# One kernel, two orders: the steps of a gated linear attention and its expert layer put in another sequence

## The chip, the cores and the metric

One core of one Trainium2 chip runs the whole program in one launch. The time is the device time of the program in microseconds (us), the median of several runs. The engines are PE (TensorE, matrix products; its weight loads are listed as PEld), DVE (VectorE), ACT (ScalarE), POOL (GpSimd) and SP (SyncE, which here issues DMA transfers).

## What is computed

For 4 sequences of 768 tokens and 8 heads of width 48, a state of 48 by 48 per head is decayed by a gate and updated by each token; the output of the heads is the input of a layer with 2048 hidden units and the activation h cos(h).

```python
f = 1.0 / (1.0 + np.exp(-f_logit))
for t in range(S):                                   # S = 768
    state = f[:, :, t, :, None] * state + np.einsum('bhd,bhe->bhde', k[:, :, t], v[:, :, t])
    y[:, :, t] = np.einsum('bhd,bhde->bhe', q[:, :, t], state)
x = y.transpose(0, 2, 1, 3).reshape(B * S, H * D)    # 3072 x 384
h = x @ w_in                                         # 3072 x 2048
out = (h * np.cos(h)) @ w_out                        # 3072 x 384
```

## The kernel before

**Pairs.** The tokens are cut into 12 pairs (0 to 11) of 256 tokens, three pairs for each of the 4 sequences; two chunks of 128 rows are worked on together, and each partition holds two tokens. Heads are handled in two halves of four (the `.0` and `.1` of a step's name; for pairs 0 and 1 the loads and gates are also cut into these halves, 192 KB each instead of 384 KB).

**Units.** The expert layer works on 13 units of tokens, the first two of 128 (both from pair 0), then eleven of 256 (unit m from 2 on uses pair m - 1). For a unit of 128 tokens one step of the first product covers 512 hidden units, for one of 256 tokens two steps do; the second product takes four steps for each block of 128 rows.

**Steps.** The program is a list of 953 steps. A step's name is its kind, its pair, unit or row block, and its part:

| kind | engine | what it does |
|---|---|---|
| f, k, q, v | SP (f0.0 from ACT) | loads of pair n |
| w0.i, w1.i | SP | load of a quarter (768 KB) of w_in, of w_out |
| wc0.i, wc1.i | POOL or ACT | the quarter cast to bf16 |
| zf | PE | filler: a product of zeros that nobody reads |
| zsp, zqk, zvt, zsz | POOL or DVE | memsets of padding in buffers |
| ex, ln, fx, fy | ACT | exp, log and the gate from f |
| ad, cum | POOL, PE | sum of the two tokens' logs; running sum by a triangular matrix |
| eb, ei | ACT | exp of the running sum, and of its negative |
| qa, ka | POOL (DVE for parts of pairs 0, 1) | first product on q, on k |
| qm, km | POOL (DVE for parts of pairs 0, 1) | decayed q and k, written to the buffer qk |
| tq, tk, qkt | PE, then DVE or ACT | transposes of q and k (pairs 5 to 11: one DMA transpose by SP, tq) |
| sc, am | PE, DVE | scores, and scores times a mask (1024 columns of PSUM) |
| vb, vt | POOL or ACT | v cast to bf16, and its four copies with padding |
| ps, st, sz | PE, DVE | new state, plus the old one, times the decay |
| y, yi, xe | PE, then DVE or ACT | output from scores and from the state; copied to x |
| h, co, g | PE, ACT, DVE | x w_in into two PSUM banks; its cosine; their product |
| o, ot, out | PE, DVE or ACT, SP or ACT | g w_out; copied out of PSUM; stored |

A few dependencies are used below. `h0.0*` and `h0.1*`, `h1.0*`, `h1.1*` read w_in by quarters: `h0.00` and `h1.00` need wc0.0, `h0.01` and `h1.01` need wc0.1, and for units of 256 tokens `hm.j*` needs wc0.j. `om.s` needs the g of its unit and wc1.s. `y0` needs all four vt of pair 0 and both am.

**Order.** Each engine runs its steps in the sequence of the text `ORDER`, and waits in each for the steps whose results, or whose buffers, it needs. A word such as `am0.1:V3` gives the step, its engine (T = PE, S = ACT, V = DVE, G = POOL, Y = SP) and the buffer places that it opens. PSUM has eight banks, 0 to 7; sc and h take two neighbouring ones. Since the queues are strict, a step that waits holds all that stand behind it on its engine. `emit` goes through the list; `apart` tells the framework which steps share a PSUM tile without sharing a bank. The line numbers in the profile of before: L264 zf, L282 w, L296 f, k, q, v, L329 to L351 gates, qa and ka, L363 ad, L374 and L380 cum, L391 and L395 eb and ei, L404 qm and km, L435 tq and tk, L456 sc, L461 am, L479 ps, L497 st, L503 sz, L531 y and yi, L561 g, L579 h, L584 co, L595 o, L606 out, and L197 for every copy and cast (wc, vb, vt, qkt, xe, ot). In the changed kernel all of them are one higher.

## Time and profile before

| | |
|---|---|
| median of 3 runs | 182.93 us (182.87 to 183.12) |
| profiled execution | span from first to last instruction 180.9 us; its device time is not listed apart, so it is set beside the median |
| granted TensorE clock | 1.00 in every slice |
| busy: PE, DVE, ACT, POOL | 172.6, 134.6, 130.7, 109.2 us |
| read from memory, written | 25.17 MB, 4.72 MB |

The profile is one execution. A group's row gives line, engine, operation, operands, count, then busy time, mean duration in ns, and the idle time of the engine just before with what ended it. Rows of the timeline and of the chain of waits begin with the start and the length in us. A row of a window gives the stretch, its length, then busy time and number of instructions for each engine, the clock, the busy share of DMA and GB/s. Matmul ends are modelled, so PE's pace is read from the spacing of its steps rather than from the length of one.

### The profile page before, as it was taken

To read this page: it belongs to the slowest core of one execution; us is meant where nothing else is said; L and a number is where in the kernel's file an instruction comes from. 1 tells how busy PE (TensorE), PEld (TensorE's weight loads), DVE (VectorE), ACT (ScalarE), POOL (GpSimd) and SP (SyncE) were. 2 spreads that over 40 slices of the span, in tenths; PEclk is the share of its full clock that TensorE was granted. 3 is DMA by queue.
4 is the path that set the end of the run, shared out by engine and by line. 5 is a ranking of instruction groups with operands and counts; after the bars stand their busy time and mean duration, and the time that the engine had idled before them with its cause. 6 is when DMAs were issued, how large, how long until landed. Compare 5 with 4: busy or idle time off the path is not lost.

```text
span 180.9 us, 5814 instructions
## 1 busy us (share of the span) xinstructions
PE 172.6 (95%) x2460; PEld 123.9 (69%) x2464; DVE 134.6 (74%) x206; ACT 130.7 (72%) x187; POOL 109.2 (60%) x139
## 2 busy tenths in 40 slices
...
DMA  5999999999999944986899999559927500110313
GB/s 149 261 261 276 343 320 341 250 318 284 301 265 233 274 83 123 252 210 145 122 180 308 173 267 278 124 131 251 203 92 182 100 4 0 43 47 4 130 43 131
DMA packets 72282, 33.93 MB, mean 188 GB/s; under 512 B 65344, under 2 KB 70720, under 8 KB 72256
## 3 DMA queue, kind: packets, MB, share of 16 engines
...
q8 instruction: 19, 0.31, 0.7%
...
HBM read 25.17 MB, written 4.72 MB: 165 GB/s over the span
## 4 chain that ended last, share of the span: by engine, by line
PE 81%; DMA 7%; ACT 3%; DVE 3%; SPq 2%; issue 1%; ACTq 0%
PE ps L595 35%; PE ps L579 33%; PE ps L531 5%; DMA f<-in_f_logit_dram 4%; PE ps L456 4%; DMA v<-in_v_dram 3%; SPq L296 2%; PE ps L479 2%; DVE g L561 1%; PE ps L435 1%; PE ps L374 1%; DVE am L461 1%; PE ps L264 1%; ACT f L344 0%; ACT f L329 0%
## 5 line engine op out<-in xcount | busy, mean ns | idle before, releaser
L561 DVE TENSOR_TENSOR g<-ps,co 128x1024 bf16<-128x1024 f32 x48 | 57.4, 1220 | 18.0 <-ACT co L584 16.7
L595 PE MATMUL ps<-w_out_bf,g 128*128 128x384 bf16 x384 | 68.9, 326 | 0.0
L579 PE MATMUL ps<-x,w_in_bf 128*128 128x256 bf16 (+1 forms) x624 | 68.1, 264 | 0.5 <-DVE x L197 0.4
L584 ACT ACTIVATE co<-ps,halfpi 128x1024 bf16<-128x1024 f32 x48 | 52.7, 1113 | 19.8 <-PE ps L579 19.5
L579 PEld LDWEIGHTS <-w_in_bf 128*128 128x128 bf16 x624 | 56.3, 98 | 9.2 <-DVE x L197 0.6
L595 PEld LDWEIGHTS <-g 128*128 128x128 bf16 x384 | 36.1, 98 | 21.4
L461 DVE TENSOR_TENSOR am<-ps,pmask 128x1024 bf16<-128x1024 f32 x24 | 28.7, 1218 | 5.2 <-PE ps L456 4.9
L404 POOL TENSOR_TENSOR qk<-k,bi 128x384 bf16<-128x384 f32 x22 | 22.0, 1008 | 5.4 <-ACT bi L391 4.7
L404 POOL TENSOR_TENSOR qk<-q,b 128x384 bf16<-128x384 f32 x21 | 20.8, 1000 | 2.7 <-DVE q L338 2.1
L197 POOL COPY vt<-vb 64x384 bf16<-64x384 bf16 x33 | 16.7, 507 | 1.6
L264 PE MATMUL ps<-zero 128*128 128x512 bf16 x50 | 14.6, 412 | 1.5 <-DVE zero L203 1.2
L503 DVE TENSOR_TENSOR sz<-ps,b 64x192 bf16<-64x192 f32 x40 | 14.1, 354 | 2.5 <-PE ps L479 1.6
L363 POOL TENSOR_TENSOR sp<-ls 128x384 bf16<-128x384 f32 x10 | 10.3, 1028 | 7.8 <-ACT ls L333 6.1
L341 POOL TENSOR_TENSOR q<-f,q 128x384 f32<-128x384 f32 x10 | 10.0, 998 | 8.0 <-DMA q<-in_q_dram 5.8
L329 ACT ACTIVATE f<-f 128x768 f32<-128x768 f32 (+1 forms) x14 | 10.4, 746 | 4.4 <-DMA f<-in_f_logit_dram 4.4
L497 DVE TENSOR_TENSOR ps<-ps,sz 64x192 f32<-64x192 f32 x32 | 11.7, 367 | 2.2 <-PE ps L479 1.1
L351 POOL TENSOR_TENSOR k<-k,f 128x384 f32<-128x384 f32 (+1 forms) x12 | 11.1, 931 | 3.4 <-DMA k<-in_k_dram 3.4
L197 ACT COPY ot<-ps 128x384 f32<-128x384 f32 (+1 forms) x14 | 6.1, 453 | 8.7 <-PE ps L595 8.7
L197 ACT CAST x<-ps 128x384 bf16<-128x384 f32 x12 | 5.5, 479 | 6.0 <-PE ps L531 6.0
L456 PE MATMUL ps<-qkt 48*64 48x128 bf16 (+1 forms) x304 | 8.7, 218 | 1.1 <-ACT x L197 0.8
L197 DVE CAST x<-ps 128x384 bf16<-128x384 f32 x12 | 6.4, 553 | 4.1 <-PE ps L531 3.9
L264 PEld LDWEIGHTS <-zero 128*128 128x128 bf16 x54 | 4.8, 103 | 5.9 <-issue 1.9
...
## 6 DMA issues: line engine op xcount, KB each, us to landing
...
```

The costliest lines, as they stand in the source:

```text
L197: (nc.scalar.copy if e == "ACT" else eng(e).tensor_copy)(out=o, in_=i)
L264: G.step(f"zf{i}", ("PE",), lambda e, dump=dump: nc.tensor.matmul(dump.ap, lhsT=zero[:, 0:128], rhs=zero, start=True, stop=True), writes=[ ...
L351: eng(e).tensor_mul(out=w.ap[:, :, 0, :], in0=w.ap[:, :, 0, :], in1=t.ap[:, :, 0, :])
L404: G.step(f"{nm}{n}.{u}", ("POOL", "DVE") if cut else ("POOL",), lambda e, u=u, j=j, src=src, dec=dec: eng(e).tensor_mul(out=qkp[u][j].ap[: ...
L456: nc.tensor.matmul(o[t0:t1, r, 2 * a + g, :].rearrange("p (e n) -> p e n", e=2), lhsT=wide[s, t0 // 64, :] if turned else wide[s].rearrang ...
L461: G.step(f"am{n}.{u}", ("DVE",), lambda e, u=u, sc=sc: nc.vector.tensor_mul(out=am[u].ap.rearrange("p r b n -> p (r b) n"), in0=sc.ap.rear ...
L497: nc.vector.tensor_add(out=view()[s], in0=view()[s], in1=S0.ap[s, :, r, :])
L503: eng(e).tensor_mul(out=new.ap[s, :, r, :].rearrange("p (u a) n -> p u a n", u=2), in0=view()[s].rearrange("p (u a) n -> p u a n", u=2), i ...
L561: nc.vector.tensor_mul(out=o.rearrange("p b (n e) -> p b n e", e=2), in0=ph.ap.rearrange("p (b e n) -> p b n e", e=2, n=64), in1=co.ap.rea ...
L579: nc.tensor.matmul(ph.ap[:, i * T:(i + 1) * T].rearrange("p (g t) -> p g t", t=C), lhsT=w_in_bf[:, kk, f0:f0 + 128], rhs=xa[:, :, kk, :], ...
L584: G.step(f"co{m}.{j}", ("ACT",), lambda e, ph=ph, co=co: nc.scalar.activation(out=co.ap, in_=ph.ap, func=AF.Sin, bias=halfpi), reads=[ph], ...
L595: nc.tensor.matmul(po.ap[:, 0:DM], lhsT=gT.ap[:, j, i * C:(i + 1) * C], rhs=w_out_bf[:, j, :], start=(po.first and j == 4 * s), stop=(po.f ...
```

## The change

The list `ORDER` is replaced by another one over the same steps, with other sequences on every engine, some steps on another engine (between DVE and ACT, POOL and ACT, POOL and DVE), and other buffer places; the number of fillers goes from 54 to 57. Nothing else is changed, and each engine's kinds of work stay nearly the same: three xe and one qkt go from DVE to ACT, one ot from ACT to DVE, one wc from ACT to POOL.

In the new list, SP issues f0, then the quarter w0.0, then k0, q0, f1.0, v0 and the rest of pair 1; w0.1 comes after v1, w0.2 and w0.3 after q3 and k3 (before: w0.1 and w0.0 together after pair 1 and f2, f3). The cast wc0.0 is the second of POOL's steps, wc0.1 follows vb1 and two vt. On PE, h0.00 comes ahead of sc1.1 and h0.01. Cut to the head of both lists, one stretch of the new one, and both ends:

```diff
-ZEROS = 54
+ZEROS = 57
...
 ORDER = """
-zvt.2:V zsp.1:V zsp.0:G zsz.3:V f0.1:Y0 f0.0:S zqk.0:G k0.0:Y0 ex0.1:S ex0.0:S k0.1:Y ln0.1:S1
-zf0:T0 zf1:T0 zf2:T0 zf3:T0 zf4:T0 zf5:T0 zf6:T0 zf7:T0 zf8:T0 zf9:T0 cum0.1:T0 ln0.0:S cum0.0:T1
-fx0.0:S ei0.1:S0 fx0.1:S ei0.0:S ka0.0:V f1.1:Y1 km0.0:G0 f1.0:Y ex1.1:S ka0.1:V zf10:T2 zf11:T2
-zf12:T2 zf13:T2 zf14:T2 zf15:T2 zf16:T2 zf17:T2 tk0.0:T2 eb0.1:S0 ex1.0:S ln1.1:S1 ln1.0:S fx1.0:S
-q0.1:Y0 q0.0:Y v0:Y0 fx1.1:S eb0.0:S qa0.1:V zqk.1:V qm0.1:V vb0:S0 f3:Y2 k1.1:Y1 km0.1:V qa0.0:V
-zf18:T3 cum1.1:T3 zf19:T4 zf20:T4 zf21:T4 tq0.1:T0 cum1.0:T1 qm0.0:G zsz.2:G eb1.0:S1 vt0.3:S2
-k1.0:Y ei1.0:S0 ex3:S zf22:T4 zf23:T4 zf24:T4 zf25:T4 zf26:T4 ps0.1:T4,5 ps0.0:T tk0.1:T v1:Y1 f2:Y0
-qkt0.1:V0 eb1.1:S ln3:S0 ei1.1:S ka1.0:G q1.0:Y0 tq0.0:T ka1.1:G km1.1:G0 zvt.1:G vt0.0:S ad3:G1
-vt0.1:G q1.1:Y vb1:S1 qkt0.0:V1 vt0.2:G zsz.1:G ex2:S w0.1:Y0 w0.0:Y1 k3:Y0 q3:Y1 w0.3:Y2 ln2:S1
-vt1.2:S1 fy3:S zf27:T6 zf28:T6 zf29:T6 zf30:T6 zf31:T6 zf32:T6 sc0.0:T0 sz0.01:V2 sz0.00:V w0.2:Y3
-ad2:G0 vt1.0:G km1.0:V vt1.3:G wc0.1:G am0.0:V0 zf33:T6 zf34:T6 yi0:T4 sc0.1:T2 am0.1:V1 st0.11:V
-sz0.11:V3 wc0.0:G k2:Y1 zf35:T6 zf36:T6 zf37:T6 zf38:T6 ps1.1:T6,7 tk1.0:T0 ps1.0:T zf39:T1 zf40:T1
-zf41:T1 cum3:T1 fy2:S ei3:S0 fx3:S ka3:G eb3:S2 vt1.1:S fx2:S km3.0:G1 qa3:G qm3.0:G km3.1:G qm3.1:G
-w1.0:Y0 qa1.0:V st0.10:V qa1.1:V qm1.0:V wc0.2:G ka2:G q2:Y2 tk1.1:T2 zf42:T3 zf43:T3 y0:T3 tq1.0:T
-xe0.1:S0 sz0.10:V st1.00:V st1.01:V qm1.1:V v2:Y1 zf44:T5 zf45:T5 zf46:T5 zf47:T5 zf48:T5 tq1.1:T
-cum2:T1 sz1.00:V1 qkt1.0:V0 eb2:S0 xe0.0:S ei2:S1 qkt1.1:V1 km2.0:G0 km2.1:G zf49:T5 sc1.0:T4
-sz1.01:V zf50:T0 zf51:T0 sc1.1:T2 h0.01:T0 st1.11:V sz1.11:V2 am1.1:V0 wc1.0:G qa2:G zf52:T6 zf53:T6
-h0.00:T co0.0:S0 qm2.1:G am1.0:V1 h1.01:T2 h1.00:T co1.0:S1 y1:T6,4 yi1:T g0.0:V1 xe1.1:V1 st1.10:V
-qm2.0:G vb2:G1 sz1.10:V g1.0:V4 w1.2:Y3 xe1.0:S tk3.0:T5 h2.01:T0 tq3.0:T w1.3:Y0 qkt3.0:V0 v3:Y0
...
-o22.1:T3 o22.2:T out16:Y o20.3:T6 o20.0:T g11.1:V o20.1:T h12.01:T o20.2:T co12.0:S0 g12.0:V o21.2:T
-o22.3:T o21.1:T o23.3:T7 o22.0:T ot20:V3 ot21:V1 out20:Y ot22.0:V2 ot22.1:V out22.0:Y out21:Y
-out22.1:Y o23.2:T o23.0:T o23.1:T ot23.0:S3 out23.0:Y ot23.1:S out23.1:S
+zsp.2:V zsp.1:G zsz.2:V f0.0:S2 f0.1:Y w0.0:Y2 zvt.1:V k0.1:Y0 q0.1:Y0 f1.0:Y0 ex0.1:S ln0.1:S1
+fx0.1:S qa0.1:V zsz.0:V ka0.1:V wc0.0:G zvt.0:G zqk.2:G zf0:T0 zf1:T0 zf2:T0 zf3:T0 zf4:T0 zf5:T0
+zf6:T0 zf7:T0 zf8:T0 zf9:T0 zf10:T0 zf11:T0 zf12:T0 zf13:T0 zf14:T0 cum0.1:T3 ei0.1:S0 eb0.1:S1
+ex0.0:S ln0.0:S zf15:T0 zf16:T0 zf17:T0 zf18:T0 zf19:T0 zf20:T0 zf21:T0 zf22:T0 cum0.0:T2 fx0.0:S
+qm0.1:V2 zf23:T0 zf24:T0 zf25:T0 zf26:T0 zf27:T0 zf28:T0 zf29:T0 zf30:T0 tq0.1:T6 q0.0:Y k0.0:Y
+qa0.0:V ei0.0:S eb0.0:S qm0.0:V km0.1:G zf31:T7 zf32:T7 zf33:T7 tq0.0:T7 tk0.1:T v0:Y0 vb0:G0
+vt0.2:G0 vt0.3:G vt0.0:G f1.1:Y ka0.0:V zqk.0:V km0.0:V zf34:T0 zf35:T0 tk0.0:T qkt0.0:V1 ex1.0:S
+ln1.0:S2 cum1.0:T5 qkt0.1:S0 zf36:T4 sc0.1:T2 am0.1:V3 f2:Y1 q1.0:Y1 ps0.1:T4,0 sc0.0:T6 ps0.0:T
+sz0.01:V2 zsp.0:V sz0.00:V zf37:T1 zf38:T1 zf39:T1 zf40:T1 zf41:T1 zf42:T1 yi0:T1 zsz.1:G fx1.0:S
+ex1.1:S qa1.0:V ei1.0:S1 eb1.0:S2 ln1.1:S fx1.1:S ex2:S cum1.1:T5 ln2:S0 ei1.1:S fx2:S qm1.0:V0
+st0.10:V am0.0:V2 st0.11:V sz0.11:V1 k1.0:Y1 ka1.0:G km1.0:G zqk.1:G zf43:T2 zf44:T2 zf45:T2 zf46:T2
+zf47:T2 zf48:T2 zf49:T2 zf50:T2 tk1.0:T7 f3:Y2 ex3:S ln3:S1 fx3:S ad2:G2 tq1.0:T qkt1.0:V2 zf51:T2
+zf52:T2 cum2:T2 eb2:S0 sc1.0:T6 k1.1:Y ka1.1:G km1.1:V q1.1:Y eb1.1:S qa1.1:V sz0.10:V qm1.1:V
+vt0.1:G zf53:T3 y0:T4 xe0.1:S2 xe0.0:S tk1.1:T0 am1.0:V0 ad3:G0 cum3:T3 v1:Y1 vb1:G2 zf54:T5 zf55:T5
+ps1.1:T5,4 vt1.3:G1 vt1.0:G ps1.0:T tq1.1:T zf56:T1 h0.00:T6 st1.00:V qkt1.1:V1 st1.01:V ei2:S1
+eb3:S1 vt1.1:S fy3:S ei3:S2 sc1.1:T0 am1.1:V1 sz1.00:V0 sz1.01:V st1.11:V st1.10:V w0.1:Y0 h1.00:T2
+wc0.1:G h0.01:T vt1.2:S y1:T0,1 yi1:T xe1.0:V0 co0.0:S3 q3:Y2 qa3:G qm3.0:G2 h1.01:T xe1.1:S
+h2.00:T0 h2.01:T g0.0:V1 sz1.11:V0 k3:Y2 tq3.0:T5 h2.10:T6 ka3:G qm3.1:G co1.0:S0 g1.0:V3 fy2:S
+sz1.10:V km3.0:G co2.0:S2 g2.0:V0 tk3.0:T qkt3.0:S2 tq3.1:T2 h2.11:T sc3.0:T4 am3.0:V2 w0.2:Y4
+wc0.2:G h2.20:T0 km3.1:G tk3.1:T h2.21:T co2.1:S1 g2.1:V h0.10:T4 qkt3.1:S3 sc3.1:T2 am3.1:V3
+w0.3:Y2 wc0.3:G h0.11:T q2:Y0 qa2:G h2.30:T6 v3:Y1 co2.2:S2 g2.2:V vb3:S2 co0.1:S3 h1.10:T2 vt3.2:S0
+h1.11:T co1.1:S0 ps3.1:T0,1 g0.1:V ps3.0:T sz3.01:V2 sz3.00:V h2.31:T co2.3:S1 qm2.1:G1 qm2.0:G
+tq2.1:T4 w1.2:Y4 wc1.2:G o3.2:T5 o2.2:T0 g1.1:V o1.2:T2 g2.3:V k2:Y1 ka2:G w1.0:Y2 wc1.0:S o0.2:T3
...
+ot0:V3 ot1:V2 tq5.0:Y1 co3.1:S3 h3.01:T4 h3.00:T co3.0:S2 h4.21:T2 g3.1:V3 h4.20:T co4.2:S0 h3.21:T
+g3.0:V h4.30:T6 co3.2:S1 g4.2:V1 g3.2:V h4.31:T co4.3:S2 h4.11:T4 h4.10:T co4.1:S3 h3.31:T2 km5.1:G
+qm5.1:G vt4.1:G vt4.2:G g4.3:V g4.1:V h3.30:T co3.3:S0 tq5.1:Y0 g3.3:V o4.1:T0 tq4.1:T7 tk4.1:T
+o5.2:T1 o4.2:T tq4.0:T6 qkt4.1:V3 tk4.0:T qkt4.0:V4 o4.0:T ps4.1:T4,5 ps4.0:T st4.01:V st4.00:V
+sc4.1:T2 am4.1:V2 sc4.0:T6 sz4.00:V0 sz4.01:V st4.11:V st4.10:V sz4.11:V3 sz4.10:V o5.3:T o5.1:T
+ex7:S o5.0:T ex6:S ln7:S0 ad7:G1 vb5:S0 vt5.2:G2 vt5.1:G ln6:S1 ad6:G2 fy6:S vb6:G1 vt4.0:G fx6:S
+ka6:G cum7:T2 eb7:S1 am4.0:V3 o6.2:T3 ei7:S1 o4.3:T ot5:S1 o6.1:T cum6:T2 eb6:S0 ot4:V0 sc5.0:T4
+am5.0:V0 yi4:T7,6 ei6:S2 fx7:S km6.1:G1 y4:T xe4.1:S2 xe4.0:S sc5.1:T0 ps5.1:T2 ps5.0:T st5.01:V
+sz5.01:V2 am5.1:V3 st5.00:V sz5.00:V o6.3:T km6.0:G h4.00:T4 h4.01:T co4.0:S1 ps6.1:T6,7 ps6.0:T
+sz6.01:V0 vt5.3:S sz6.00:V vt5.0:G vt6.1:G1 h5.00:T0 h5.01:T y5:T6,2 yi5:T xe5.1:S1 xe5.0:S qa6:G
+g4.0:V o6.0:T h5.30:T4 st6.10:V sz6.10:V1 vt6.3:G qm6.1:G v7:Y0 vb7:G2 k7:Y0 qm6.0:G q9:Y2 ka7:G
...
+h12.20:T6 h12.21:T co11.1:S3 co12.2:S0 o21.2:T0 g11.3:V o21.0:T o20.0:T1 o21.3:T g11.1:V o20.1:T
+h12.31:T4 h12.30:T co12.3:S2 h12.10:T2 g12.2:V4 g12.3:V h12.01:T6 h12.00:T o21.1:T h12.11:T
+co12.1:S0 g12.1:V o20.2:T o23.2:T4 o22.3:T5 o20.3:T o22.2:T co12.0:S1 o22.1:T g12.0:V o22.0:T
+ot22.1:V3 ot20:S1 o23.1:T out22.1:Y ot22.0:S out20:Y o23.3:T o23.0:T ot23.0:V0 out22.0:S ot21:S2
+out21:Y ot23.1:S out23.1:Y out23.0:S
"""
```

100 lines of the change are left out of this document (42 added, 58 removed).

## The prediction

> **What bounds the kernel now.** I read the page of the profile first, then the busy time by window, then the chain of waits between 24 and 40 us.
>
> ```profile
> span 180.9 us, 5814 instructions
> PE 172.6 (95%) x2460; PEld 123.9 (69%) x2464; DVE 134.6 (74%) x206; ACT 130.7 (72%) x187; POOL 109.2 (60%) x139
> DMA  5999999999999944986899999559927500110313
> L264 PE MATMUL ps<-zero 128*128 128x512 bf16 x50 | 14.6, 412 | 1.5 <-DVE zero L203 1.2
> ...
> 24.77:50.00 25.23, 24.56 (x397) 18.82 (x397) 20.65 (x24) 19.80 (x20) 24.14 (x28) 1.00 1.09 303
> 50.00:177.60 127.60, 127.59 (x1828) 94.51 (x1816) 97.12 (x135) 91.58 (x125) 70.66 (x87) 1.00 0.66 152
> ...
> 24.77 0.84 PE L579 MATMUL ps<-x,w_in_bf 128*128 128x128 bf16 x12
> 29.70 0.83 PE L579 MATMUL ps<-x,w_in_bf 128*128 128x256 bf16 x6 [0.42 <-DVE x L197]
> ```
>
> The window rows (after the stretch: its length, PE, PEld, DVE, ACT, POOL, clock, DMA, GB/s) say nearly all. From 50.00 to 177.60 PE is busy 127.59 of 127.60 us at full clock, and that is matrix work in a fixed amount. So the change can gain nothing there, only lose. Before 24.77 PE turns over fillers (14.6 us of L264) while DMA is full and the others prepare pairs 0 and 1. At 24.77 the first expert step, h0.01, starts, and from 29.70 (h2.01) the stream is dense but for small holes. The time is: start of the stream, plus fixed PE work, plus tail. The span of 180.9 is 2.0 under the median of 182.93; I take that distance as fixed and add differences to 182.93.
>
> ```profile
> 27.95 1.23 DVE g L561
> 29.18 0.48 DVE x L197
> 29.68 0.37 DVE ps L497
> 30.07 0.35 DVE sz L503
> 32.64 1.24 DVE am L461
> 36.06 0.33 PE ps L456 x8
> ```
>
> In the chain, between 27.95 and 33.9 it is VectorE that sets the pace, and only then PE.
>
> **The change, part 1: the head.** The amount of work is the same (three fillers more, ten table loads in both); order and buffers alone differ. I walk the queues of the new order, each step starting when its queue and its inputs allow, with these durations:
>
> ```profile
> 4.28 0.94 ACT L329 ACTIVATE f<-f 128x384 f32<-128x384 f32 x2 [1.76 <-DMA f<-in_f_logit_dram]
> 8.41 0.36 DVE L338 SCALAR_TENSOR_TENSOR q<-f,q 128x192 f32<-128x192 f32 x1 [1.12 <-DMA q<-in_q_dram]
> 10.67 0.83 ACT L197 CAST vb<-v 128x768 bf16<-128x768 f32 x1 [0.79 <-DMA v<-in_v_dram]
> 24.00:28.00 4.00, 4.00 (x64) 3.13 (x64) 2.89 (x5) 3.07 (x4) 3.92 (x4) 1.00 1.07 346
> ...
> L461 DVE TENSOR_TENSOR am<-ps,pmask 128x1024 bf16<-128x1024 f32 x24 | 28.7, 1218 | 5.2 <-PE ps L456 4.9
> L404 POOL TENSOR_TENSOR qk<-k,bi 128x384 bf16<-128x384 f32 x22 | 22.0, 1008 | 5.4 <-ACT bi L391 4.7
> L197 POOL COPY vt<-vb 64x384 bf16<-64x384 bf16 x33 | 16.7, 507 | 1.6
> L197 POOL CAST vb<-v 128x768 bf16<-128x768 f32 x9 | 7.4, 824 | 0.9 <-PE ps L479 0.7
> L584 ACT ACTIVATE co<-ps,halfpi 128x1024 bf16<-128x1024 f32 x48 | 52.7, 1113 | 19.8 <-PE ps L579 19.5
> L197 DVE COPY qkt<-ps 128x1024 bf16<-128x1024 bf16 x7 | 4.6, 681 | 2.9 <-PE ps L435 2.9
> 22.18 2.87 POOL L197 CAST w_in_bf<-g 128x1536 bf16<-128x1536 f32 x2
> 28.44 0.51 PE L531 MATMUL ps<-qkt,sz 128*32 128x128 bf16 x24
> ```
>
> DMA first. Between the waits ended at 8.41 (q0.1) and 10.67 (v0) three halves of 192 KB landed: 0.75 us each, 1.5 a whole. A 768 KB quarter at 346 GB/s takes 2.3; that window also holds the slower small loads, so I take 2.1 (2.3 would cost 0.2 more). SP's queue now has w0.0 third, ahead of pair 0's k, q and v. Landings: f0 4.7, w0.0 6.8, k0.1 7.5, q0.1 8.3, q0.0 9.8, k0.0 10.5, v0 12.0 (10.67 before), k1.0 15.8, k1.1 18.0, v1 20.3, w0.1 22.4. SP is not held: its one slot wait there, f3 for ka0.0, ends by 12.
>
> Then a resource which the durations of before already show:
>
> ```profile
> 9.38 0.55 DVE L404 TENSOR_TENSOR qk<-k,bi 128x384 bf16<-128x384 f32 x1
> 14.36 0.93 DVE L404 TENSOR_TENSOR qk<-k,bi 128x384 bf16<-128x384 f32 x1
> 13.73 1.14 POOL L351 TENSOR_TENSOR k<-k,f 128x192 f32<-128x192 f32 x2 [2.06 <-DMA k<-in_k_dram]
> 14.96 1.19 POOL L404 TENSOR_TENSOR qk<-k,bi 128x384 bf16<-128x384 f32 x1
> 19.48 0.54 DVE L404 TENSOR_TENSOR qk<-q,b 128x384 bf16<-128x384 f32 x1
> 19.57 1.31 POOL L363 TENSOR_TENSOR sp<-ls 128x384 bf16<-128x384 f32 x1 [0.52 <-ACT ls L333]
> ```
>
> The same DVE product takes 0.55 alone and 0.93 while POOL's ka1.1 (to 14.87) runs; the POOL product behind it takes 1.19 instead of 1.0; ad2, started 0.09 after a DVE product, 1.31 instead of 1.0. In each the second behaves as if begun about 0.14 before the first one's end. So DVE's qa, ka, qm, km and POOL's steps that read SBUF exclude each other. The Trainium skill (SBUF — State Buffer, "Who interferes with whom") has the rule: a VectorE instruction with two SBUF inputs and a GpSimd one that reads SBUF hold a shared port for the whole instruction, first come first served. The rows agree but for that 0.14. By the skill's whole instructions the five handovers from vt0.1 to qm1.1 below would be 0.7 dearer and the sum 183.2.
>
> The walk. POOL: wc0.0 6.8 to 8.3, two memsets, km0.1 behind DVE's qm0.1, 9.5 to 10.5. DVE: qa0.0 behind that 10.4, then qm0.0, ka0.0, a memset and km0.0 to 12.4. POOL: vb0 to 13.0, three vt and a memset to 15.0, waits for k1.0, ka1.0 to 16.4. DVE: qkt0.0 to 13.5, am0.1 14.8, two sz 15.6, qa1.0 15.9, qm1.0 behind ka1.0 16.8. POOL: km1.0 17.7, memset 18.2, ad2 19.1, ka1.1 19.7, vt0.1 20.2. DVE: st, am0.0, st, sz to 19.1, qkt1.0 19.7, km1.1 behind vt0.1 to 20.6. Handover by handover: ad3 to 21.4, qa1.1 21.7, vb1 22.3, qm1.1 22.8, vt1.3 23.1. POOL: vt1.0 23.6, wc0.1 (half of 2.87) 25.1. DVE: am1.0 to 23.9, which frees the banks of h0.00: 23.95. st1.00 and qkt1.1 to 24.9, so sc1.1 24.95, h1.00 25.3, h0.01 25.95 (wc0.1 is there at 25.1). am1.1 25.4 to 26.6, y1 26.65, two sz, yi1 27.35, h1.01 27.75; yi1's end and the two xe (0.2 and 0.55 behind) give h2.00 at 28.7 to 28.8. Before, h2.01 stood at the same place of the work at 29.70, with tk3.0 (0.22) done besides. Lead: 29.70 - 0.22 - 28.8 = 0.7. The chain goes through DVE and POOL, not DMA. Without the six late collisions h2.00 would be at 28.0 (lead 1.5); had POOL won all of them, at 29.9 (0.4 behind).
>
> **Part 2, 29 to 50 us.** DVE stays in charge: g0.0, g1.0, g2.0, am3.0, g2.1, am3.1, g2.2, g0.1 follow back to back at 1.2 each. By the same walk PE waits for g1.0 (tq3.1, 0.35), qkt3.0 on ACT, g2.0 (0.3 together), am3.1 (0.1), g0.1 (0.15), g1.1 (0.4), sz2.01 (0.1): 1.4. From 29.70 the old order lost 0.67 less the 0.42 in the row at 29.70 as idle time, and, by the spacing of its steps in the timeline, about 1 more (an estimate). I take 0.1 lost, bounds -0.4 (the old holes were larger than shown) and +0.5.
>
> **Part 3, the dense part.** Here there is only something to lose. The tightest place I find in the order is DVE between g3.0 and g4.0, which o6.0 needs:
>
> ```profile
> 75.88 1.31 PE ps L579 x12
> 87.18 2.60 PE ps L595 x16
> 122.08 0.90 PE ps L531 x56
> 63.08 0.89 PE ps L435 x16
> 58.39 2.36 DVE L561 TENSOR_TENSOR g<-ps,co 128x1024 bf16<-128x1024 f32 x2 [0.29 <-ACT co L584]
> ```
>
> Between h3.00 and o6.0 PE has 13 h steps (0.655), 11 o steps (0.65), two y with yi (0.9), four transposes (0.89), four sc (0.25 to 0.33) and eight ps and cum (0.2, an estimate from their spacing): 20.9 us. From that come off 1.4 until co3.0 has made g3.0's input: 19.5. DVE has 7 g at 1.18, 4 am at 1.22, 2 qkt, 14 st and sz at 0.37 and one ot (0.5): 20.2. So o6.0 would stand 0.7 late; consecutive am overlap a little as g do, which takes off up to 0.4. I take 0.4, bounds 0 and 0.8. Elsewhere I find each wait for co, g, am or a transpose covered by as much PE work as before, and take nothing.
>
> **Part 4, the tail.**
>
> ```profile
> 171.58 6.01 PE L595 MATMUL ps<-w_out_bf,g 128*128 128x384 bf16 x36
> 177.63 0.54 ACT L197 COPY ot<-ps 128x192 f32<-128x192 f32 x2 [4.74 <-PE ps L595]
> 178.20 0.36 ACTq L606 DMA_DIRECT2D out_dram<-ot  x1
> ```
>
> After the last matmul ACT made both halves of ot23 one after the other, 0.54 to the issue. Now DVE makes one and ACT the other: 0.25 saved. ot21 and an issue lie on ACT before it, but they fit under o23.1, o23.3 and o23.0 (1.95). If not, up to 0.3 is lost.
>
> **Sum.** 182.93 - 0.7 + 0.1 + 0.4 - 0.25 = 182.5.
>
> **Rivals.** (B) The collisions come out milder, as one engine is done before the other starts: lead 1.5, and no lateness at o6.0: 181.3. For it: two of the DVE products in the rows above, at 9.38 and 19.48, kept their 0.55. Against: in my walk POOL is without a gap from 15.8 to 42, so nearly every DVE product meets it. (C) A handover lasts from the first one's very end, 0.14 later than the rows let me think: five of them on the way to am1.0 take the lead of 0.7 back, 183.2, no change. (D) Slower: POOL gets the shared reads first at km0.0, qa1.0 and qa1.1, so that vb0, km1.0 and vb1 (0.8 to 1.0 each) go ahead of DVE; that moves am1.0 to 25.1 and h2.00 to 29.9. With parts 2 to 4: 182.93 + 0.4 + 0.1 + 0.4 - 0.25 = 183.6. It decides once h2.00 is later than 29.2. For it: at all three the two engines are ready within 0.3 us of each other. Against: at 14.36 a waiting DVE step did win over POOL's next. (E) The change does not do what it says: with w0.0 third, pair 0 is not whole ahead of it, and if the quarter, sharing DMA with f0.0 of ACT's queue, delays what follows by 1.0 more than its 2.1, the lead turns into 0.3 behind: 183.5.
>
> **How the numbers follow.** The forecast has 0.38, B 0.14, C 0.10, D 0.33, E 0.05. A measurement tells about 0.2% (0.37 us) from no change. Faster: B and four fifths of the forecast (0.31), 0.45. Within: the rest of the forecast (0.07) and most of C (0.07), 0.14. Slower: D, E and the rest of C, 0.41. The range goes from B with its tail (181.2) to D with the upper end of part 3 and some of part 2 (184.2). The forecast's own range is 182.0 to 182.9.
>
> **What would show it.** Right: am1.0's end near 23.9, h2.00 near 28.8, POOL without a gap from 16, DVE km1.1 and POOL ad3 and vb1 lengthened by 0.2 to 0.4, a small PE hole at o6.0, none larger behind it. Wrong: h2.00 outside 28.2 to 29.3, a PE hole of over 0.5 after 60 us, or a wait for a load or a transpose where I saw none.

## The result, and the profile after

The changed kernel takes **185.09 us** (median; 184.08 to 186.24), the kernel before 182.90 beside it (182.60 to 183.12): a ratio of 1.0121, 95% interval 1.0096 to 1.0145. It is slower by 2.2 us, where 182.5 with a range of 181.2 to 184.2 was forecast. Its times also spread over 2.2 us, those of before over 0.5. The profiled execution took 185.07 us with a span of 183.3, 2.4 longer than before.

From the page of the changed kernel:

```profile
span 183.3 us, 5826 instructions
PE 175.0 (95%) x2467; PEld 125.8 (69%) x2467; DVE 135.1 (74%) x205; ACT 132.0 (72%) x189; POOL 109.5 (60%) x138
PE 86%; DVE 9%; issue 2%; ACT 1%; DVEq 0%
```

And its busy time by window, cut at the first expert step, at 50 us and behind the last matmuls (length, PE, PEld, DVE, ACT, POOL, clock, DMA, GB/s):

```profile
24.50:50.00 25.50, 24.63 (x380) 18.85 (x369) 22.84 (x33) 22.34 (x27) 21.45 (x23) 1.00 1.04 297
50.00:179.40 129.40, 129.13 (x1851) 95.91 (x1849) 95.09 (x128) 93.37 (x129) 72.30 (x87) 1.00 0.66 150
179.40:183.30 3.90, 0.15 (x1) 0.00 (x0) 0.36 (x1) 0.32 (x1) 0.00 (x0) 1.00 0.48 168
```

TensorE still looks full behind 50 us (0.27 us idle against 0.01). A busy share doesn't show how far the work has come, so I count that: for a step in the dense part, its start less the TensorE work that stands ahead of it, each kind of step with one fixed duration in both kernels. This lag grows by whatever was lost. The columns are the us of TensorE work ahead of the step at which it is read; the last one is the span's end less the last o step's start (all in us):

```
work done      10      50      62      75      97     152    end
before      19.87   21.31   21.87   22.56   22.74   23.53   4.09
after       20.45   21.88   22.86   23.56   24.14   25.48   4.55
```

So the 2.4 us are 0.6 at the head (to h2.00, which stands at 30.07), nothing from there to 50 us, 0.4 up to o6.0, 0.95 in the rest of the dense part and 0.45 behind it. The waits of TensorE in the changed kernel name only the first of these places:

```profile
PE ps L436 <- DVE am L462: 1.0, 1, 1.0
PE ps L436 <- DVE sz L504: 0.8, 1, 0.8
PE ps L532 <- issue: 0.7, 1, 0.7
```

The first is tk1.0's wait for a bank behind am0.0 at 19.5 us, the second one like it (tk1.1) at 23.1. The third has no releaser: TensorE stopped inside yi1 with nothing that the profile shows to wait for.

### The profile page after: what moved, and what is told of

Same layout as the page of the kernel before. It is cut to its first block, busy times and chain, and to the rows that moved or that the text cites. A ratio compares the mean times of both kernels' runs of the same rounds, so it can differ in the third digit from the quotient of the medians.

```text
span 183.3 us, 5826 instructions
## 1 busy us (share of the span) xinstructions
PE 175.0 (95%) x2467; PEld 125.8 (69%) x2467; DVE 135.1 (74%) x205; ACT 132.0 (72%) x189; POOL 109.5 (60%) x138
## 4 chain that ended last, share of the span: by engine, by line
PE 86%; DVE 9%; issue 2%; ACT 1%; DVEq 0%
PE ps L580 34%; PE ps L596 31%; PE ps L265 6%; PE ps L532 5%; PE ps L457 4%; DVE am L462 3%; PE ps L436 2%; DVE ps L498 2%; DVE sz L504 2%; PE ps L480 2%; DVE qk L405 1%; DVE q L339 1%; PE ps L375 1%; ACT co L585 1%; PE ps L381 0%
## 5 line engine op out<-in xcount | busy, mean ns | idle before, releaser
L405 POOL TENSOR_TENSOR qk<-q,b 128x384 bf16<-128x384 f32 x20 | 19.8, 999 | 0.6
L265 PE MATMUL ps<-zero 128*128 128x512 bf16 x57 | 16.6, 427 | 1.2 <-DVE zero L204 1.2
L198 ACT CAST x<-ps 128x384 bf16<-128x384 f32 x15 | 6.8, 479 | 10.6 <-PE ps L532 10.5
L198 DVE COPY ot<-ps 128x384 f32<-128x384 f32 (+1 forms) x13 | 6.7, 522 | 7.5 <-PE ps L596 7.1
L265 PEld LDWEIGHTS <-zero 128*128 128x128 bf16 x57 | 5.5, 107 | 7.3 <-issue 3.0
L457 PE MATMUL ps<-qkt 48*64 48x128 bf16 (+1 forms) x304 | 9.2, 220 | 0.4 <-DVE qkt L198 0.3
```

The source lines that it names most:

```text
L198: (nc.scalar.copy if e == "ACT" else eng(e).tensor_copy)(out=o, in_=i)
L265: G.step(f"zf{i}", ("PE",), lambda e, dump=dump: nc.tensor.matmul(dump.ap, lhsT=zero[:, 0:128], rhs=zero, start=True, stop=True), writes=[ ...
L405: G.step(f"{nm}{n}.{u}", ("POOL", "DVE") if cut else ("POOL",), lambda e, u=u, j=j, src=src, dec=dec: eng(e).tensor_mul(out=qkp[u][j].ap[: ...
L457: nc.tensor.matmul(o[t0:t1, r, 2 * a + g, :].rearrange("p (e n) -> p e n", e=2), lhsT=wide[s, t0 // 64, :] if turned else wide[s].rearrang ...
```

## The experiments

Steps are named as above, and a ratio is the time over that of the kernel before, measured beside it. Where two engines don't collide, single steps last as long as in the changed kernel; what differs is when they come. The line numbers in the rows are each kernel's own: those with a shorter list have the numbers of before (L435, L197) again.

**The old last copies.** ot21 on VectorE, both halves of ot23 on ScalarE, out23.0 by SyncE:

```
-ot23.0:V0 out22.0:S ot21:S2 out21:Y ot23.1:S out23.1:Y out23.0:S
+ot21:V2 out22.0:S out21:Y ot23.0:S0 out23.0:Y ot23.1:S out23.1:S
```

> The changed kernel with the last copies of the kernel before: ot21 on VectorE, both halves of ot23 on ScalarE, out23.0 issued by SyncE. In the trace of the changed kernel ScalarE's ot23.1 starts at 179.98, only when VectorE's ot23.0 (179.58 to 179.94) is done, although they read and write different columns; the last output is issued 0.77 us behind the last matmul, against 0.61 before, and the span ends 2.96 behind that issue, against 2.67. Theory 1 (the halves on two engines go one after the other, so the edit costs instead of saving): the last issue comes 0.61 behind the last matmul again, last matmul to end 3.3 as before instead of 3.73, time 184.7. Rival (the later end is set by the transfers, which are as many): 3.7 again, 185.1. The rest of the kernel is untouched, so the idle stretch of TensorE inside yi1 at 28.3 to 29.2 should be there again if it belongs to the order, and be gone or elsewhere if it is chance.

Measured: 184.37 (183.70 to 186.26), ratio 1.0082 (1.0049 to 1.0115). The timelines of the end, first of the changed kernel, then with the old copies:

```profile
179.58 0.36 DVE L198 COPY ot<-ps 128x192 f32<-128x192 f32 x1 [1.59 <-PE ps L596]
179.98 0.32 ACT L198 COPY ot<-ps 128x192 f32<-128x192 f32 x1 [0.71 <-DVE ot L198]
```

```profile
178.46 0.54 ACT L198 COPY ot<-ps 128x192 f32<-128x192 f32 x2 [1.24 <-PE ps L596]
179.03 0.34 ACTq L607 DMA_DIRECT2D out_dram<-ot  x1
```

On one engine the two halves overlap (0.54 for both); on two engines the second begins when the first is done. The last issue comes 0.61 behind the last matmul instead of 0.77: 0.16 of the tail, as theory 1 had it. The span still ended 3.0 behind that issue, so the tail as a whole isn't back at that of before. The runs spread as widely as without the edit. More telling is the head, which this edit doesn't touch: h2.00 stood at 28.94, not 30.07, and the stop in yi1 was gone. Here are VectorE and GpSimd at 15.5 to 18.3 us, changed kernel first:

```profile
15.90 0.75 DVE L339 SCALAR_TENSOR_TENSOR q<-f,q 128x192 f32<-128x192 f32 x1
16.75 1.18 DVE L405 TENSOR_TENSOR qk<-q,b 128x384 bf16<-128x384 f32 x1
15.85 0.59 POOL L352 TENSOR_TENSOR k<-k,f 128x192 f32<-128x192 f32 x1 [0.88 <-ACT f L348]
16.52 1.00 POOL L405 TENSOR_TENSOR qk<-k,bi 128x384 bf16<-128x384 f32 x1
```

```profile
15.64 0.34 DVE L339 SCALAR_TENSOR_TENSOR q<-f,q 128x192 f32<-128x192 f32 x1
16.09 0.77 DVE L405 TENSOR_TENSOR qk<-q,b 128x384 bf16<-128x384 f32 x1
15.75 0.69 POOL L352 TENSOR_TENSOR k<-k,f 128x192 f32<-128x192 f32 x1 [0.87 <-ACT f L330]
16.52 1.20 POOL L405 TENSOR_TENSOR qk<-k,bi 128x384 bf16<-128x384 f32 x1
```

These are qa1.0 and qm1.0 on VectorE, ka1.0 and km1.0 on GpSimd. The rows name steps of ScalarE as what ka1.0 waited for, but the one that it needs, fx1.0, was done 2 us before; the last part of k1.0 landed 0.13 before ka1.0 both times. If VectorE reaches qa1.0 before ka1.0 starts (15.64 against 15.75), qa1.0 and qm1.0 go first and am1.0 ends at 24.00; if it comes after (15.90 against 15.85), km1.0 goes ahead of qm1.0 and am1.0 ends at 24.73. Up to the tail the two programs are the same, so the same head runs in both ways.

**One memset moved**, to let VectorE go first:

```
-ka1.0:G km1.0:G zqk.1:G
+ka1.0:G zqk.1:G km1.0:G
```

> The changed kernel with one memset (zqk.1) put on GpSimd between ka1.0 and km1.0 instead of behind them, so that VectorE's qm1.0 finds GpSimd busy with something that reads no SBUF and goes first. In the trace of the changed kernel km1.0 started at 16.52, ahead of qm1.0, which took 1.18 us (16.75 to 17.93) instead of about 0.6. Theory 1 (the shared reads of VectorE and GpSimd decide the head, rival D of the prediction): qm1.0 ends near 17.2, am0.0 starts 0.7 earlier, km1.1 and what follows lie differently, am1.0 ends 0.4 to 0.8 before 24.73 and h2.00 as much before 30.07; 184.3 to 184.7. Rival (the later landing of k1.1 at 19.1 holds ka1.1 and all behind it): am1.0 unchanged within 0.2, 185.1. Second rival (the idle 0.9 us inside yi1 sets h2.00, whatever comes before): am1.0 earlier, h2.00 not.

Measured: 184.15 (183.79 to 184.47), ratio 1.0068 (1.0053 to 1.0083). h2.00 at 28.87, am1.0's end at 23.93, and the spread fell from 2.2 to 0.7 us. The gain is 0.9 and not 0.4 to 0.8, as the stop in yi1 went too. In the profiled run VectorE came first in any case (qa1.0 at 15.58, ka1.0 at 15.72), so that trace doesn't test the memset; that it settles the race rests on the spread.

**Twenty instructions more on TensorE**, ten of the fillers cut into two halves each (`dump.ap[:, a:b]` for 0 to 256 and 256 to 512).

> The changed kernel with the first ten fillers cut into two matmuls of 256 columns each: the same columns, 20 instructions more on TensorE ahead of everything. In the trace of the changed kernel TensorE stands idle from 28.28 to 29.16 inside yi1, after 20 of its 24 matmuls, and the profile names no wait; a packet of 16 KB of instructions was moved at 26.85 to 27.78. Theory 1 (the hole is TensorE waiting for its next instructions): a hole of like size comes 20 instructions, that is ten matmuls, earlier in the work (inside y1 or at yi1's start), or, if the packet comes at another time, is gone, and then h2.00 stands up to 0.9 earlier, 184.2. Rival (yi1's last matmuls wait for data or a bank): hole at the same four matmuls, same length, 185.1.

Measured: 184.88 (184.08 to 186.20), ratio 1.0117 (1.0086 to 1.0149). No stop in yi1, but one of 0.79 inside y7. By itself this decided nothing; the next runs did.

**Steps of one shape together:**

```
-sc7.1:T6 am7.1:V1 y6:T3,5 sc7.0:T0 am7.0:V0 vt7.3:S yi6:T
+sc7.1:T6 am7.1:V1 sc7.0:T0 am7.0:V0 y6:T3,5 vt7.3:S yi6:T
-sc11.0:T0 yi10:T2,7 am10.1:V2 y10:T sc11.1:T4
+yi10:T2,7 am10.1:V2 y10:T sc11.0:T0 sc11.1:T4
-ps11.0:T6 qm11.0:G vt11.1:G y9:T0,1 yi9:T ps11.1:T
+qm11.0:G vt11.1:G y9:T0,1 yi9:T ps11.0:T6 ps11.1:T
```

> The changed kernel with three pieces of TensorE's order put together by the shape of their matmuls, late in the kernel where I see no wait on them: sc7.1 sc7.0 y6 yi6 instead of sc7.1 y6 sc7.0 yi6; yi10 y10 sc11.0 sc11.1 instead of sc11.0 yi10 y10 sc11.1; y9 yi9 ps11.0 ps11.1 instead of ps11.0 y9 yi9 ps11.1. In both traces a step followed by one with another tile shape takes 0.07 to 0.10 us more than followed by its like (h to h 0.655, h to y 0.748; o to o 0.650, o to sc 0.743; y to yi 0.457, y to o 0.554). From h3.00 on the changed order has 40 such changes, before 37; this kernel has 36. Theory 1 (each change of shape costs 0.09): 0.37 less between h6.30 and the end, 184.7. Rival (the extra time in the late part is waits on VectorE): no change, 185.1; steps next to the regrouped ones become longer by what is saved.

Measured: 184.74 (183.37 to 186.02), ratio 1.0103 (1.0067 to 1.0139). The total says little, for a stop of 1.38 us came inside h6.00 (below). At the places themselves the lag grew by 0.47 less than without the edit. TensorE in the changed kernel, and the same stretch regrouped (in a later run on a steadier head):

```profile
96.90 0.42 PE L457 MATMUL ps<-qkt 48*64 48x128 bf16 x16
97.25 0.63 PE L532 MATMUL ps<-am,vt 128*32 128x128 bf16 x32
97.81 0.42 PE L457 MATMUL ps<-qkt 48*64 48x128 bf16 x16
98.16 0.35 PE L532 MATMUL ps<-qkt,sz 128*32 128x128 bf16 x12
98.44 0.82 PE L596 MATMUL ps<-w_out_bf,g 128*128 128x384 bf16 x4
```

```profile
96.26 0.65 PE L456 MATMUL ps<-qkt 48*64 48x128 bf16 x32
96.84 0.63 PE L531 MATMUL ps<-am,vt 128*32 128x128 bf16 x32
97.29 0.34 PE L531 MATMUL ps<-qkt,sz 128*32 128x128 bf16 x12
97.57 0.82 PE L595 MATMUL ps<-w_out_bf,g 128*128 128x384 bf16 x4
```

The shape is the pair behind the operands (48*64, 128*32, 128*128). From sc7.1 to o8.3 it takes 1.54 us with four changes of shape and 1.31 with two: 0.11 each, near the 0.09 between other steps (from an h step to the next step 0.655 if that is h, 0.748 if it is y).

**The stops.** TensorE's timelines around three of them, in the changed kernel, with the shapes regrouped, and with eight fillers fewer (next experiment):

```profile
28.00 0.50 PE L532 MATMUL ps<-qkt,sz 128*32 128x128 bf16 x20
29.16 0.24 PE L532 MATMUL ps<-qkt,sz 128*32 128x128 bf16 x4 [0.66 <-issue]
```

```profile
100.98 0.72 PE L580 MATMUL ps<-x,w_in_bf 128*128 128x256 bf16 x5
102.81 0.61 PE L580 MATMUL ps<-x,w_in_bf 128*128 128x256 bf16 x4 [1.11 <-issue]
```

```profile
78.65 0.40 PE L531 MATMUL ps<-am,vt 128*32 128x128 bf16 x15
79.92 0.45 PE L531 MATMUL ps<-am,vt 128*32 128x128 bf16 x17 [0.87 <-issue]
```

They stand in different steps (yi1, h6.00, y5) and in the middle of them. But counting from the start, windows that end inside each stop hold these numbers of matmuls and weight loads (first and second count):

```profile
0.00:29.10 29.10, 25.10 (x351) 14.41 (x351) 20.96 (x52) 20.12 (x39) 20.17 (x33) 1.00 1.06 273
```

```profile
0.00:102.70 102.70, 97.77 (x1502) 68.83 (x1502) 82.76 (x140) 85.25 (x128) 80.35 (x103) 1.00 1.04 250
```

```profile
0.00:79.80 79.80, 73.83 (x1118) 51.37 (x1118) 64.51 (x115) 65.19 (x98) 65.52 (x85) 1.00 1.10 262
```

From 702 to 2236 to 3004 instructions are 1534 and 768, six and three times 256 within two. The run with twenty instructions more stopped at the same number (x1502) and so in another step, y7. TensorE's instructions come in packets of 16 KB over the DMA engines; the page of the changed kernel lists them:

```profile
q8 instruction: 19, 0.31, 0.7%
```

Nineteen packets for some 4950 instructions are one for every 256. From the start and length of each packet and the start of the first matmul of its block (numbered with the records that the windows leave out); the margin is the second time less the first, the stop what TensorE stood still there:

```
kernel                    packet ends   first of block    margin   stop
changed                      27.78      706 at  29.16      1.38    0.88
shapes regrouped             27.77      706 at  29.19      1.42    1.05
shapes regrouped            101.34     3010 at 102.81      1.47    1.38
fillers cut                  99.49     3010 at 100.89      1.41    0.79
eight fillers fewer          78.49     2242 at  79.92      1.43    1.09
ten ahead, memset            77.77     2242 at  79.23      1.47    0.56
old last copies              25.61      706 at  27.55      1.94    none
before                       24.31      706 at  28.57      4.26    none
before                       98.75     3010 at 101.19      2.43    none
```

Six of the long stops end 1.4 to 1.5 us behind the end of a packet, with the first instruction of its block: TensorE had run out of instructions. In no trace does a block start less than 1.29 behind its packet's end, and three stood at 1.33 to 1.41 without a stop of over 0.1. Some short stops (0.2 to 0.7) had margins of 1.5 to 2.3 and fit less well. Before had at least 2.4 us in hand at every block.

**Eight fillers fewer and eight more** ahead of cum0.1:

```
-zf7:T0 zf8:T0 zf9:T0 zf10:T0 zf11:T0 zf12:T0 zf13:T0 zf14:T0 cum0.1:T3
+cum0.1:T3                       (eight fewer; eight more: zf0 to zf22 stand there)
```

> The changed kernel without eight of its fillers (zf7 to zf14, of the fifteen that stand ahead of cum0.1 on TensorE; 49 fillers in all). In the profiles so far the fillers ran slowly (0.42 us each instead of 0.215) for a time that differs from run to run: none in the run with cut fillers, 7 in the run with the moved memset, 10 in the run with the old tail, 11 in the changed kernel, 13 in the regrouped one. With them cum0.1 starts at 5.81, 5.98, 6.47, 6.73, 7.23 and h2.00 at 29.20, 28.87, 28.94, 30.07, 30.09: the two runs in which cum0.1 came after 6.5 are those in which ka1.0 (behind the landing of k1.0, 15.7) beat qa1.0, and km1.0 qm1.0, on the port. Theory 1 (the fillers at the slow clock decide the race): cum0.1 near 5.6 in every run, h2.00 near 28.9, times 183.6 to 184.3 with no run above 184.6 for this reason, median 183.9 to 184.1. Rival (the order of the head's port is chance, or the clock needs the fillers): spread 183.7 to 186.3 and median 184.9 as without the edit.

> The changed kernel with eight more fillers ahead of cum0.1 (23 instead of 15; 65 in all). Theory 1 (fillers decide the race): cum0.1 after 7.3 in every run, am0.1 after 14.3, ka1.0 and km1.0 go ahead, h2.00 at 30.0 or later, times 185.0 to 186.5, median 185.3 or more. Rival (chance): as the changed kernel, 184.1 to 186.2 around 185.0, with some runs near 184. Of the instructions: the stream is 16 instructions longer ahead of yi1. The idle stretch of 0.88 and 1.05 us in yi1 came at instruction 706 of TensorE both times, the one of 1.38 in h6.00 (regrouped kernel) and the one of 0.79 in y7 (cut fillers, where the stream is 20 longer) at instruction 3010, which is nine times 256 later, each ending 1.38 to 1.47 after the end of a 16 KB packet of instructions. If it is the fetch, a hole in this run stands again at instruction 706, now eight matmuls earlier in yi1, and ends 1.4 after the packet; if it is yi1's data, it stands where it stood.

Measured: eight fewer 184.30 (183.98 to 185.93), ratio 1.0073 (1.0043 to 1.0103); eight more 186.47 (185.26 to 187.78), ratio 1.0179 (1.0139 to 1.0220). In the head theory 1 holds in both: h2.00 at 29.07, and at 31.63. With eight more VectorE comes to qa1.0 only at 16.74, when km1.0 is under way, so qa1.0 loses too (1.16 instead of 0.34) and am1.0 ends at 26.69. Of the spread theory 1 doesn't hold: with eight fewer some runs took 184.9 to 185.9, and the profiled one had lost 1.09 us at instruction 2242. The fillers ahead of cum0.1 in the timeline of TensorE, in the changed kernel, with shapes regrouped, and with eight more (start, length in all, count at the end):

```profile
1.19 5.70 PE L265 MATMUL ps<-zero 128*128 128x512 bf16 x15 [1.19 <-DVE zero L204]
```

```profile
1.19 6.21 PE L265 MATMUL ps<-zero 128*128 128x512 bf16 x15 [1.19 <-DVE zero L204]
```

```profile
1.19 6.55 PE L265 MATMUL ps<-zero 128*128 128x512 bf16 x23 [1.19 <-DVE zero L204]
```

The same fifteen fillers last 5.70 in one run and 6.21 in another: the first 11 of them at 0.42 each in the one, the first 13 in the other, 10 with the old last copies, 7 with the moved memset, and 0.215 for the rest. (The clock column shows 1.00 here throughout; that the clock is what makes them slow is inferred from a filler of the run with all edits below, which takes 0.43 at 25.80, where the column shows 0.50.) (The run with cut fillers was slow up to 3.9 us, its halves taking 0.21; what the expectation on record says, none slow, misread that.) Ten fillers are done by 5.4 even when all are slow, when cum0.1's input has just come; fifteen are not, and cum0.1 came at 6.73 and 7.23. Eight more put it at 7.57 though only 7 of them were slow. The stop at 706 did not come with eight more (margin 4.41), so what was expected of its place found no answer in that run.

**Two sums that failed.** With eight fillers fewer and the regrouped shapes, the order of the dense part was mended where I saw waits:

```
-ot5:S1 o6.1:T cum6:T2 eb6:S0 ot4:V0             +ot5:S1 ot4:S0 o6.1:T cum6:T2 eb6:S0
-st5.01:V sz5.01:V2 am5.1:V3 st5.00:V            +am5.1:V3 st5.01:V sz5.01:V2 st5.00:V
-co4.0:S1 ... vt5.3:S                            +vt5.3:S ... co4.0:S1
-sz7.11:V3 ... sz7.10:V am6.1:V3                 +am6.1:V3 sz7.11:V3 ... sz7.10:V
-st9.10:V ... st8.00:V ... st9.11:V sz8.00:V     +st8.00:V sz8.00:V st9.10:V ... st9.11:V
```

> The kernel with eight fillers fewer, the three regroupings by shape, and the waits taken out that I see in the dense part of the changed kernel: ot4 on ScalarE instead of VectorE, am5.1 ahead of st5.01 and sz5.01, vt5.3 ahead of co4.0 on ScalarE (for y5 and o6.0); am6.1 ahead of sz7.11 and sz7.10 (for sc7.1); st8.00 and sz8.00 ahead of st9.10 and st9.11 (for o13.1's bank). Theory 1 (shape changes and VectorE's order are what the dense part loses, 0.76 more than before by the trace, of which holes of 0.12, 0.21, 0.18 and 0.22, and three changes of shape at 0.09): against the kernel with eight fillers fewer -0.45 by shape and -0.4 to -0.6 by the waits: 183.0 to 183.2. Rival (the waits move on to the next step of VectorE): only the 0.45, 183.5.

> All edits together: eight fillers fewer, the memset between ka1.0 and km1.0, the regroupings and the order of the dense part, and the last copies: ot21 on VectorE, the halves of ot23 in two buffers of their own, one on VectorE and one on ScalarE, out23.0 issued by SyncE and out23.1 by ScalarE. Theory 1: both halves of ot23 start together, the last issue 0.40 behind the last matmul instead of 0.77 (0.61 with both on ScalarE), -0.35 for the tail; with the rest 182.6 to 182.9, equal to the kernel before or 0.3 faster. Rival (copies of one bank by two engines go one after the other even in buffers of their own): -0.15 for the tail, 182.9 to 183.1.

Measured: 184.68 (184.28 to 185.49), ratio 1.0088 (1.0061 to 1.0115), and 185.05 (184.57 to 185.73), ratio 1.0102 (1.0077 to 1.0127). In the first, h7.30 and h7.20 waited 0.5 each behind ot8, which stood on VectorE until the store of ot4 had left its buffer; 0.34 went at instruction 2242. In the profiled run of the second the head was late once more, for another reason. Its TensorE at 23 us, and its clock (last but two) in two windows:

```profile
23.09 0.53 PE L435 MATMUL ps<-ident,qk 128*128 128x128 bf16 x4 [1.19 <-DVE sz L503]
```

```profile
20.00:24.00 4.00, 2.49 (x57) 1.75 (x55) 3.97 (x6) 2.21 (x6) 3.80 (x6) 0.90 1.20 306
24.00:26.00 2.00, 2.00 (x41) 1.07 (x38) 1.04 (x2) 1.91 (x4) 1.63 (x2) 0.50 0.96 317
```

Behind an idle stretch of 1.19 the granted clock stood at half for some 3 us, and h0.00 came at 26.22 though am1.0 was done at 24.68. But the five other runs of this kernel had a mean granted clock of 1.000 and took 184.57 to 185.73 all the same, so the fall of the clock doesn't explain the median, and what does stays open. Nor is it shown that the missing fillers brought it about: the first sum and the run with eight fillers fewer have as few of them and kept the full clock there. Its last copies went to two buffers, and still one after the other:

```profile
179.66 0.36 DVE L197 COPY ot<-ps 128x192 f32<-128x192 f32 x1 [1.13 <-PE ps L595]
180.05 0.32 ACT L197 COPY ot<-ps 128x192 f32<-128x192 f32 x1 [1.63 <-DMA out_dram<-ot]
```

The row names a store, the last event by the profile; but both buffers are new places that no earlier step used, so no store holds them. So it is the PSUM bank that both read, not the buffer.

**A ladder, and loads moved.** Ten fillers ahead of cum0.1 (zf10 to zf14 out) with the moved memset; then loads out of the bursts; then shapes; then the rest:

```
-k7:Y0 q9:Y2 out5:Y f9:Y2 q7:Y1 tq6.1:Y0 f8:Y1 tq6.0:Y4 out6:Y q8:Y0 ... v9:Y0 f10:Y0 tq8.0:Y0 tq8.1:Y1
+k7:Y0 out5:Y q7:Y1 tq6.1:Y0 f8:Y1 tq6.0:Y4 f9:Y2 out6:Y q8:Y0 q9:Y2 ... tq8.0:Y0 tq8.1:Y1 v9:Y0 f10:Y0
```

> First step of a ladder: the changed kernel with five fillers fewer ahead of cum0.1 (ten, as many as before had; 52 in all) and the memset between ka1.0 and km1.0. With eight fewer the runs were 183.98 to 185.93, median 184.3, h2.00 at 29.07 and an idle 1.09 us at instruction 2242; with eight more 185.26 to 187.78, median 186.47. With eight fewer and all other edits the granted clock fell to 0.5 from 24 to 26, behind an idle stretch of 1.19. Theory 1 (fillers that come late cost, missing ones risk the clock): cum0.1 at 5.6 to 5.9, clock 1.0 from 9 us on, qm1.0 ahead of km1.0, h2.00 28.8 to 29.1, median 183.9 to 184.2. Rival (the head is not what differs): 184.9 and a spread of 2 us.

> Second step: also the loads q9, f9, v9 and f10 issued later on SyncE (f9 behind tq6.0, q9 behind q8, v9 and f10 behind tq8.1), which the changed order has in two bursts of 265 to 320 GB/s at 70 to 77 and 96 to 101 us; nobody needs them before 91, 109, 109 and 112. In the runs so far the packet for instructions 2242 on starts at 75.5 to 77.4 and the one for 3010 on at 97.6 to 100.7, inside these bursts; the idle stretches come in the runs in which less than 1.5 us are left between its end and its use. Theory 1 (the packets wait behind loads): both packets start earlier against the work, margins at 2242 and 3010 above 2 us, no idle stretch there, 0.2 to 0.4 less than the step before in the median and a smaller spread. Rival (packets come when the engine asks, whatever else is under way): margins and idle stretches as before.

> Third step: also the three regroupings by shape (four changes of shape fewer). Theory 1 (0.09 each): 0.37 to 0.47 less than the second step. Rival (waits take it back): the same time.

> Fourth step: also the order of the dense part (ot4 on ScalarE, am5.1 ahead of st5.01, vt5.3 ahead of co4.0, am6.1 ahead of sz7.11, st8.00 and sz8.00 ahead of st9.10) and the last copies of the kernel before. Theory 1 (holes of 0.12, 0.18 and 0.22 on TensorE go, 0.15 at the end): 0.5 to 0.65 less than the third step; the sum of the ladder is 182.7 to 183.1, at the kernel before or 0.2 faster. Rival (each hole comes back at the next wait, as in the run with the dense edits, where ot8 then waited for out4): 0.2 less.

Measured: 183.99 (183.71 to 184.60), ratio 1.0055 (1.0037 to 1.0074); then 186.46, 186.69 and 186.08, ratios 1.0194, 1.0199 and 1.0170 (intervals within 0.003 of each). The first step did what was expected: h2.00 at 28.95 and a spread of 0.9. The moved loads cost 2.5: q9 ahead of v10, out1 and the transposes made these late, out4 landed at 101.8 instead of 99.1, and ot8 and sc9.0 waited (0.9 and 1.3). The last rung names such waits:

```profile
PE ps L456 <- DMA qkt<-qk: 2.4, 2, 1.9
```

At instruction 2242, though, the margin rose from 1.47 to between 1.9 and 2.4 in all three, with 0.17 or less idle. At 3010 it didn't: the last two rungs stopped there for 0.6, and the last one at 706 for 0.9, again 1.3 to 1.4 behind a packet's end.

**The terms one by one**, each on the first rung: three transfers moved with no one behind them hurt (f9 behind tq6.0, out4 behind out6, q9 behind f10); the shapes alone; the dense order alone with out4 early; and all, with the old last copies.

> The kernel with ten fillers ahead of cum0.1 and the moved memset (183.99), with f9 issued behind tq6.0, out4 early (behind out6) and q9 late (behind f10). In w2_spread the margin at instruction 2242 rose from 1.47 to 2.24 and the idle stretch there was gone, but out4 landed at 101.8 instead of 99.1 and ot8 and h7.30 waited for it, and the transposes tq9 came later. Theory 1 (the packet waits behind the loads): margin at 2242 above 1.9, nothing idle there (0.56 in the kernel it is built on), no new wait at h7.30 and sc9.0; 183.5 to 183.8. Rival (the packet's time is chance): margins between 1.4 and 2.4 as before, 184.0.

> The kernel with ten fillers ahead of cum0.1 and the moved memset (183.99), with the three regroupings by shape alone. Theory 1 (0.09 for each of four changes of shape): 183.5 to 183.65. Rival (waits take it back, sc7.0 waits for tq7.0 or for its bank): 183.8 to 184.0.

> The kernel with ten fillers ahead of cum0.1 and the moved memset (183.99), with the order of the dense part alone (ot4 on ScalarE, am5.1 ahead of st5.01, vt5.3 ahead of co4.0, am6.1 ahead of sz7.11, st8.00 and sz8.00 ahead of st9.10), and out4 issued early so that ot8 need not wait for its buffer. Theory 1 (the holes of 0.12, 0.18 and 0.22 at y5, sc7.1 and o13.1 were VectorE's order): they are gone, 183.4 to 183.6. Rival (they move on): 183.8 to 184.0.

> All that helped together: ten fillers, memset, loads as in x1_loads, regroupings by shape, order of the dense part, the last copies of the kernel before. Theory 1 (the terms add up: -0.3 loads, -0.4 shape, -0.5 waits, -0.15 last copies): 182.6 to 182.9, at the kernel before or up to 0.25% faster. Rival (new waits take half of it back): 183.3.

Measured, against before at 183.30 beside them: loads 184.19 (183.50 to 184.79), ratio 1.0059 (1.0038 to 1.0080); shapes 184.36, ratio 1.0052 (1.0035 to 1.0070); dense order 183.69, ratio 1.0027 (1.0011 to 1.0042); all 183.12 (182.27 to 185.57), **ratio 0.9996 (0.9973 to 1.0019)**. The loads brought the margin at 2242 to 2.22 and the stop from 0.56 to 0.15, but no gain in the median. The shapes saved 0.45 where they are, and a stop of 0.67 at instruction 3010 hid it in the profiled run; the median shows no gain. The dense order removed its three holes; from 50 us to the end of the stream TensorE, in the window of that kernel, is never idle:

```profile
50.00:177.90 127.90, 127.90 (x1824) 95.21 (x1812) 93.88 (x125) 92.76 (x129) 71.69 (x87) 1.00 0.68 152
```

All together the kernel is level with before, not ahead. Its lags at the six places are 19.33, 20.76, 21.36, 21.82, 22.52 and 23.63: the lead of 0.5 at the head is there, and the stretch from 75 us on takes it back.

**One instruction more on GpSimd** (a memset of a spare tile at the start, on the first rung):

> The kernel with ten fillers ahead of cum0.1 and the moved memset (183.99; end of the span 2.98 behind the last output's issue, GpSimd's step between two semaphores of the final barrier 0.39), with one small memset more on GpSimd, at the start where it waits anyway: 203 instructions of GpSimd instead of 202. Theory 1 (the step depends on where the end stands in GpSimd's instructions, so on their number): 0.08 or 0.09 and an end 2.6 to 2.7 behind the last issue, 183.7. Rival (it goes with the moved loads, which the other kernels with 203 had): 0.37 to 0.39, 184.0.

Measured: 183.76 (183.49 to 184.23), ratio 1.0032 (1.0019 to 1.0045). The step was 0.09 and the end came 2.62 behind the last issue, not 2.98: theory 1. Why 202 instructions are worse than 203 or 208 stays open. The kernels with moved loads, the one with all terms among them, have 203 too, so 0.3 us of their difference from the first rung is this step and nothing that they were built for.

## Why the prediction was wrong

**The head (forecast -0.7, measured +0.6).** The step that failed is the walk's start: up to qa1.0 it follows DMA, GpSimd and VectorE and gives TensorE's fillers no time at all. It put qa1.0 at 15.6 to 15.9 and ka1.0 from 15.8, VectorE 0.2 us ahead; the other order was rival D, with a chance of 0.33, but no part of the forecast had the fillers as what decides between the two. Fifteen fillers ahead of cum0.1, whose pace doubles anywhere between 3.7 and 7.0 us, move am0.1 by up to 0.8 and decide that race. Where VectorE wins, the walk is right to 0.1 or 0.2 (am1.0 24.00 against 23.9, h2.00 28.94 against 28.8, which is the forecast lead of 0.5 to 0.6). Where it loses, rival D comes true in part (am1.0 24.73 against 25.1), and with it the packet of instructions came late (27.78 against 25.61): D's 29.9 for h2.00 was nearly met, at 30.07, but by 0.4 us less of D and a stop of 0.9 that no part of the forecast had. The Trainium skill (TensorE: Matmul & The Clock Gate, "Part 1: The HAM clock gate") says that the number of slow matmuls at the start differs from run to run, 6, 11 or 14 for one kernel, and advises against fitting it. The rows agree, with 7 to 13; but here an order that needs ten or fewer loses 0.7 at am1.0 when there are more, and 1.1 at h2.00 with the stop, so the worst count has to be walked, not the mean.

**29 to 50 us (forecast +0.1).** Measured 0.0: the lag grows by 1.44 before and 1.43 after. This shows the net alone: the wait forecast at tq3.1 (0.35) stands in the profile as 0.19 of idle time, and the others weren't compared one by one.

**The stretch to o6.0 (forecast +0.4).** Measured 0.42, but the agreement is luck. The place that the forecast named, o6.0 behind g4.0, didn't wait. The changed kernel has g4.0, vt5.3, y5 and o6.0 like this:

```profile
79.33 1.21 DVE L562 TENSOR_TENSOR g<-ps,co 128x1024 bf16<-128x1024 f32 x1
79.00 0.51 ACT L198 COPY vt<-vb 64x384 bf16<-64x384 bf16 x1
79.65 0.88 PE L532 MATMUL ps<-am,vt 128*32 128x128 bf16 x32
80.80 0.82 PE L596 MATMUL ps<-w_out_bf,g 128*128 128x384 bf16 x4
```

g4.0 was done at 80.54 and o6.0 followed on yi5 at 80.80. What the stretch lost is 0.12 at y5, whose last input to come was ScalarE's vt5.3 (done at 79.51), a pause of 0.21 inside y5 at instruction 2242, which I can't put down to the packet for sure (margin 2.33), and the price of one more change of shape (12 against 11), 0.09. So VectorE's sum of 20.2 against TensorE's 19.5, the term that gave the 0.4, stands behind none of these.

**Behind o6.0 (forecast 0, measured +0.95).** That each wait elsewhere is covered was wrong three times (sc7.1 0.18, o13.1 0.22, o14.1 0.08), each time through a bank that VectorE freed late; I had looked only for co, g, am and transposes. Three more changes of shape (29 against 26) are 0.28 by the rows. The rest is spread over differences below 0.1 that I didn't trace. The premise under this, that a stream without idle time is a fixed amount of work, doesn't hold: four changes of shape fewer took 0.45 out of it, so there was something to gain as well as to lose.

**The tail (forecast -0.25, measured +0.45).** Two engines don't copy out of one bank at once: +0.16 instead of -0.25. The Trainium skill (PSUM — Partial Sum Buffer, "PSUM bank collisions raise a hardware error") has the rule: two engines on the same bank and partitions collide, reads too, and the compiler puts a dependency between them. The rows agree (179.58 to 179.94, then 179.98). The other 0.29 is GpSimd's step in the final barrier (0.37 against 0.08), which no row of before could have shown.

**What held:** DVE and POOL excluding each other with the second begun about 0.14 early (in the changed kernel qm1.0 ended at 17.93: km1.0's end at 17.52, less 0.14, and 0.55), and the landings of w0.0 to v0 within 0.5 us (rival E fell).
